# Three loads of v issued by ScalarE's queue instead of SyncE's, in a lightning-attention and MLP kernel

## Chip, cores and metric

The kernel runs on one core of one Trainium2 chip. The metric is the device time of one execution in microseconds (us); a number for a kernel is the median of its runs, in most cases four. A ratio is the mean time of one kernel's runs over the mean of the other's runs of the same rounds on the same chip, so it is not quite the ratio of the medians that are quoted; its 95% interval stands in brackets. The span in a profile is about 2 us shorter than the time of the same run. All times "at" a moment are us from the start of the span.

## The reference

A decayed linear attention over q, k and v of shape (4, 8, 768, 64), then an MLP with the tanh form of gelu over the 3072 x 512 result. Cut to what matters:

```python
# attention, in blocks of 64 rows, for each batch and head
intra = (qb @ kb.T) * Dmask                    # Dmask[i, j] = lam**(i-j) for i >= j
out   = intra @ vb + (qb * lam_pow) @ kv_state
kv_state = lam**64 * kv_state + (kb * rev_pow).T @ vb
...
x = out.transpose(0, 2, 1, 3).reshape(3072, 512)
# MLP
h = x @ w_in                                   # (512, 2048)
g = gelu_tanh(h)
return g @ w_out                               # (2048, 512), float32
```

## The kernel before

The attention is done in 24 steps; a step is 256 rows of four heads of one batch, and needs three loads (q, k, v) of 256 KB each, whose rows in memory are 512 bytes long. The weights are loaded in pieces whose rows are 2 KB long. SyncE issues nearly all of it, in this order: q, k, v of steps 0 to 3, w_in, w_out, q, k, v of steps 4 to 8. Only the small load of lam and v of step 0 go through ScalarE's queue.

```python
def load_step(s, names="qkv"):
    ...
        t = ld.tile([P, HH, 2, D], FP32, tag=nm + "32", name=f"{nm}32_{s}")
        rows = src[b, half * HH : (half + 1) * HH, sb * SB : (sb + 1) * SB, :]
        queue = nc.scalar if (nm, s) == ("v", 0) else nc.sync
        pin(queue.dma_start(out=t[:].rearrange("p h j d -> p h (j d)"),
                            in_=rows.rearrange("h (p j) d -> p h (j d)", j=2)))
...
def load_win(j, part=None):                    # part: half of the rows, for j = 0 and 1
    ...
    cs = slice(0, NC) if part is None else slice(2 * part, 2 * part + 2)
    pin(nc.sync.dma_start(out=t[:, cs, :], in_=src[:, cs, :]))
...
for s in range(4):
    load_step(s)
for j in range(4):
    for part in ((0, 1) if j < 2 else (None,)):
        load_win(j, part)
for j in (0, 2, 1, 3):
    load_wout(j)
for s in range(4, 9):
    load_step(s)
```

A step's inputs are then prepared: VectorE scales q (GpSimd does it in step 3), ScalarE casts k to 16 bits, GpSimd scales v into 16 bits. `stage_t` transposes q and k on TensorE and copies the result out of its banks; `scores`, `causal` and `products` follow. `idle(n)` issues n matmuls of no use, 0.22 us each at full clock, that keep TensorE busy. The front of the kernel, which is what the change touches:

```python
idle(4); prep(0); stage_t(0); idle(1)
square(5); square(6)
prep(1)
chunk_decay()
idle(2); R(0, None); stage_t(1); idle(5); U(0); prep(2)
scores(1); products(1, 0); causal(1); idle(1); stage_t(2); prep_qk(3)
...
idle(3); scores(2); products(2, None); update(2, 0); causal(2)
prep_v(3)                       # GpSimd: needs v of step 3
...
stage_t(3); products(None, 1); products(None, 2); ...
scores(3)
banks = products(3, None)       # TensorE: needs prep_v(3)
cast_win(0, 0, 256, 128, c01)   # VectorE: needs the first piece of w_in
...
queue_group(0)
fill(8)                         # TensorE: the first matmuls of the MLP
```

Each engine runs its instructions in this order. So the first MLP matmul can not start before `products(3, None)`.

## Time and profile before

| | before |
|---|---|
| median of runs | 204.0 us (203.85 to 204.35) |
| span of the profiled run | 202.2 us |
| TensorE busy | 194.2 us, 96% |
| first MLP matmul at | 16.82 us |
| second block of MLP matmuls at | 19.69 us |
| v of step 3 landed at | 13.76 us |
| cast of k of step 1 at | 7.57 us |

TensorE is nearly full from 17 us on, so the table follows the front only. The last two rows of TensorE to compare with later (the timeline of TensorE before; start, length, engine, line, operation, tiles, shapes, count, and in brackets the idle time before with what ended it):

```profile
16.82 2.36 PE L601 MATMUL Hps<-xT,w_in 128*128 128x256 f16 x20 [0.56 <-DVE w_in L108]
19.69 5.20 PE L601 MATMUL Hps<-xT,w_in 128*128 128x256 f16 x28
```

The first MLP matmul ended an idle time of 0.56 us, and what ended that was VectorE's cast of w_in.

### The profile page before, as it was taken

To read this page: it belongs to the slowest core of one execution; us is meant where nothing else is said; L and a number is where in the kernel's file an instruction comes from. 1 tells how busy PE (TensorE), PEld (TensorE's weight loads), DVE (VectorE), ACT (ScalarE), POOL (GpSimd) and SP (SyncE) were. 2 spreads that over 40 slices of the span, in tenths; PEclk is the share of its full clock that TensorE was granted. 3 is DMA by queue.
4 is the path that set the end of the run, shared out by engine and by line. 5 is a ranking of instruction groups with operands and counts; after the bars stand their busy time and mean duration, and the time that the engine had idled before them with its cause. 6 is when DMAs were issued, how large, how long until landed. Compare 5 with 4: busy or idle time off the path is not lost.

```text
span 202.2 us, 5666 instructions
## 1 busy us (share of the span) xinstructions
PE 194.2 (96%) x2348; PEld 130.1 (64%) x2348; DVE 145.7 (72%) x293; ACT 107.9 (53%) x205; POOL 66.3 (33%) x80
## 2 busy tenths in 40 slices
PE   6888999999999999999999999999999999999993
PEld 1456544456888888645688764589664688544882
DVE  5896623889999999967799749899566462334753
ACT  2475778375893473477642368614367424466210
POOL 6594123457458264162531609303302000000000
PEclk9999999999999999999999999999999999999999
DMA  5999999999999999999875999306510003300014
GB/s 170 291 327 387 387 387 378 286 291 320 334 239 216 272 233 235 210 277 200 205 182 127 243 285 218 45 0 138 132 51 3 0 0 107 104 0 0 3 45 163
DMA packets 64201, 37.85 MB, mean 187 GB/s; under 512 B 17584, under 2 KB 59568, under 8 KB 64176
## 3 DMA queue, kind: packets, MB, share of 16 engines
q1 hardware_dynamic: 63344, 36.97, 72.1%
q10 hardware_dynamic: 832, 0.52, 0.8%
q8 instruction: 18, 0.29, 0.6%
q14 instruction: 7, 0.06, 0.1%
HBM read 27.26 MB, written 6.29 MB: 166 GB/s over the span
## 4 chain that ended last, share of the span: by engine, by line
PE 81%; DVE 6%; SPq 4%; DMA 4%; ACT 2%; issue 2%; DVEq 0%
PE Hps L484 37%; PE MB L555 8%; PE MA L555 8%; PE MD L555 7%; SPq L70 4%; PE MC L555 4%; DMA wi<-in_moe_w_in_dram 4%; PE Hps L601 3%; PE O2ps L499 3%; PE S L295 3%; DVE w_sum L128 2%; PE OK L353 2%; PE OK L344 1%; PE Tps L266 1%; DVE gs L531 1%
## 5 line engine op out<-in xcount | busy, mean ns | idle before, releaser
L484 PE MATMUL Hps<-xT,w_in 128*128 128x512 f16 (+1 forms) x416 | 78.7, 346 | 0.0
L488 ACT ACTIVATE gT<-Hps 128x512 f16<-128x512 f32 x88 | 52.3, 597 | 29.1 <-PE Hps L484 28.3
L484 PEld LDWEIGHTS <-w_in 128*128 128x128 f16 x416 | 40.4, 98 | 33.7
L531 DVE TENSOR_TENSOR gs<-gT 128x1024 f16<-128x1024 f16 (+1 forms) x62 | 40.8, 712 | 18.3 <-ACT gT L488 18.3
L456 POOL TENSOR_TENSOR u<-t,lumask 128x256 f16<-128x256 f32 x40 | 29.4, 749 | 67.0 <-DVE t L449 49.6
L555 PEld LDWEIGHTS <-gs 128*128 128x128 f16 x400 | 39.0, 98 | 4.5
L305 DVE TENSOR_TENSOR PT<-S,mask 128x512 f16<-128x512 f32 x48 | 30.4, 682 | 9.5 <-PE S L295 9.5
L230 POOL TENSOR_TENSOR v<-v,dv 128x512 f16<-128x512 f32 x24 | 28.5, 1194 | 5.0 <-DMA v<-in_v_dram 4.5
L555 PE MATMUL MA<-w_sum,gT 128*128 128x256 f16 x160 | 19.5, 273 | 0.4 <-DVE o L587 0.3
L555 PE MATMUL MB<-w_out,gs 128*128 128x256 f16 x160 | 19.1, 273 | 0.0
L248 ACT ACTIVATE qk<-k 128x512 f16<-128x512 f32 x24 | 15.0, 625 | 7.6 <-DMA k<-in_k_dram 7.6
L562 ACT ACTIVATE m<-MB 128x512 f32<-128x512 f32 x10 | 6.0, 597 | 23.4 <-PE MB L555 23.4
L555 PE MATMUL MD<-w_sum,gs 128*128 128x256 f16 x152 | 18.4, 273 | 0.0
L555 PEld LDWEIGHTS <-gT 128*128 128x128 f16 x160 | 15.4, 98 | 3.5 <-ACT gT L488 0.5
L243 DVE TENSOR_TENSOR qk<-q,dq 128x512 f16<-128x512 f32 x23 | 17.6, 767 | 0.0
L430 ACT ACTIVATE xT<-OK 128x256 f16<-128x256 f32 x29 | 11.1, 453 | 8.2 <-PE OK L353 7.9
L499 PE MATMUL O2ps<-w_out,gT 128*128 128x512 f16 x64 | 14.6, 379 | 0.0
L566 DVE TENSOR_TENSOR o<-MA,m 128x512 f32<-128x512 f32 x10 | 6.9, 689 | 9.6 <-ACT m L562 9.6
L128 DVE TENSOR_TENSOR w_sum<-w_out 128x1024 f16<-128x1024 f16 x10 | 9.1, 947 | 6.3 <-POOL w_out L118 3.5
L430 ACT ACTIVATE xT<-O 128x256 f16<-128x256 f32 x18 | 6.4, 458 | 10.4 <-PE O L404 7.5
L295 PEld LDWEIGHTS <-qkT 64*64 64x64 f16 x384 | 6.0, 106 | 7.0 <-issue 3.2
L449 DVE SCALAR_TENSOR_TENSOR t<-t,lamu,OK 128x64 f32<-128x64 f32 x44 | 10.1, 273 | 0.5
(68 smaller groups left out, 168.8 us busy)
## 6 DMA issues: line engine op xcount, KB each, us to landing
q<-in_q_dram SPq DMA_DIRECT2D x24, 256.0 KB, 5.3
k<-in_k_dram SPq DMA_DIRECT2D x24, 256.0 KB, 5.2
v<-in_v_dram SPq DMA_DIRECT2D x23, 256.0 KB, 5.2
out_dram<-o SPq DMA_DIRECT2D x22, 256.0 KB, 4.5
wo<-in_moe_w_out_dram SPq DMA_DIRECT2D x4, 1024.0 KB, 9.6
wi<-in_moe_w_in_dram SPq DMA_DIRECT2D x4, 512.0 KB, 7.6
wi<-in_moe_w_in_dram SPq DMA_DIRECT2D x2, 1024.0 KB, 12.7
v<-in_v_dram ACTq DMA_DIRECT2D x1, 256.0 KB, 4.4
```

The source lines that it names most:

```text
L128: pin(eng.tensor_tensor(w_sum16[:, w_slot[m], 4 * j : 4 * j + 4, :], rows(f0, e0), rows(f1, e1), op))
L230: pin(nc.gpsimd.tensor_tensor(wide(tv[:]), ld32[s][2][:], decay(dv, s), ALU.mult))
L243: pin(q_eng.tensor_tensor(wide(tq), q32[:], decay(dq, s), ALU.mult))
L248: pin(nc.scalar.activation(out=wide(tk), in_=k32[:], func=AF.Copy))
L305: pin(nc.vector.tensor_tensor(t[:, hl].rearrange("p b c d -> p b (c d)"), Sps[:].rearrange("p b c d -> p b (c d)"), mask[:].unsqueeze(1).t ...
L430: pin(nc.scalar.activation(out=d, in_=o, func=AF.Copy))
L456: pin(nc.gpsimd.tensor_tensor(u[:], state[half][:].unsqueeze(2).to_broadcast([P, 2, 2, D]), lumask[:, 2 * half : 2 * half + 2, :].unsqueez ...
L484: pin(nc.tensor.matmul(by_block(Hps[:, i, :]), w_in16[:, c, f * P : (f + 1) * P], x(c), start=(c == 0), stop=(c == NC - 1)))
L488: pin(nc.scalar.activation(out=dst, in_=Hps[:], func=AF.Gelu_apprx_tanh))
L499: pin(nc.tensor.matmul(O2[tau][0][:], gT[:, f % HF, f // HF, tau * P : (tau + 1) * P], w_out16[:, f, :], start=(n == 0), stop=(n == NF - 1)))
L531: pin(nc.vector.tensor_tensor(gsum[m][:, i, :], block(T0, F0, i), block(T1, F1, i), op))
L555: pin(nc.tensor.matmul(dst, lhsT, rhs, start=(i == 0), stop=(i == HF - 1), skip_group_check=True))
```

## The change

The intent is to take issues off SyncE, so that w_in is asked for earlier, and to let v come through a second queue beside q and k. v of step 1 follows v of step 0 at the top. v of steps 2 and 3 are issued later, each behind a cast of k on ScalarE, and land in buffers of the output pool, which is unused then.

```diff
     ld32 = {}
+    v_ahead = {}
+
+    def load_tile(nm, s):
+        first = nm == "v" and s in (2, 3)
+        return (otp if first else ld).tile([P, HH, 2, D], FP32, tag="o32" if first else nm + "32",
+                                           name=f"{nm}32_{s}")
...
-            t = ld.tile([P, HH, 2, D], FP32, tag=nm + "32", name=f"{nm}32_{s}")
+            t = v_ahead.pop(s, None) if nm == "v" else None
+            if t is None:
+                t = load_tile(nm, s)
...
-            queue = nc.scalar if (nm, s) == ("v", 0) else nc.sync
+            queue = nc.scalar if nm == "v" and s < 4 else nc.sync
...
-    for s in range(4):
-        load_step(s)
+    load_step(0)
+    load_step(1)
+    for s in (2, 3):
+        load_step(s, "qk")
+        v_ahead[s] = load_tile("v", s)
...
     prep(0)
+    load_step(2, "v")
...
     prep(1)
+    load_step(3, "v")
```

## The prediction

> **What bounds the kernel now.** I read the page first. TensorE is busy 96% of the span, and its first four slices (5 us each) are the only ones clearly under nine tenths.
>
> ```profile
> span 202.2 us, 5666 instructions
> PE 194.2 (96%) x2348; PEld 130.1 (64%) x2348; DVE 145.7 (72%) x293; ACT 107.9 (53%) x205; POOL 66.3 (33%) x80
> PE   6888999999999999999999999999999999999993
> DMA  5999999999999999999875999306510003300014
> GB/s 170 291 327 387 387 387 378 286 291 320 334 239 216 272 233 235 210 277 200 205 182 127 243 285 218 45 0 138 132 51 3 0 0 107 104 0 0 3 45 163
> ```
>
> So after about 17 us the order of TensorE's own work sets the end, and what this change can move is the front: steps 0 to 3 of the attention, and the arrival of the first quarter of w_in. The DMA row says that the transfer engines are full from about 2.4 us on; the rate row says that loads of q, k and v run at about 290 GB/s and weights at about 387.
>
> Second, the chain that ended last, in order of time (start, length, what). It goes through SyncE's twelve issues, the load of w_in and its cast into the first matmul of the MLP.
>
> ```profile
> 8.46 0.83 SPq L70
> 9.33 7.12 DMA wi<-in_moe_w_in_dram
> 16.47 0.30 DVE w_in L108
> 16.82 2.36 PE Hps L601 x20
> ```
>
> It looks as if fewer issues ahead of 9.33 would bring w_in sooner. I do not believe that, for an issue of 0.83 us is about what 256 KB take at 290 GB/s (262144 / 290e3 = 0.90 us): SyncE waits there for room, not for its own work.
>
> Third, the timeline of ScalarE in the front (start, length, what, idle before).
>
> ```profile
> 1.82 1.28 ACT L184 ACT_TABLE_LOAD   x1 [1.82 <-issue]
> 5.12 0.63 ACT L248 ACTIVATE qk<-k 128x512 f16<-128x512 f32 x1 [1.81 <-DMA k<-in_k_dram]
> 7.57 0.63 ACT L248 ACTIVATE qk<-k 128x512 f16<-128x512 f32 x1 [1.81 <-DMA k<-in_k_dram]
> 8.69 1.02 ACT L273 ACTIVATE qkT<-Tps 128x1024 f16<-128x1024 f16 x1 [0.49 <-PE Tps L266]
> 10.26 0.63 ACT L248 ACTIVATE qk<-k 128x512 f16<-128x512 f32 x1 [0.55 <-DMA k<-in_k_dram]
> 12.99 0.63 ACT L248 ACTIVATE qk<-k 128x512 f16<-128x512 f32 x1 [0.78 <-DMA k<-in_k_dram]
> ```
>
> All four casts of k wait for their load: the front runs at the pace of arrivals. The waits by engine say the same of v: GpSimd waited 4.5 us for v in three waits, the longest 1.7 us, while ScalarE lost 7.6 us to k in six. In the timeline the front's last matmuls of TensorE end at about 16.3 us and the first MLP matmul starts at 16.82, after a cast that had waited for w_in until 16.45. The two paths therefore end within 0.5 us of each other. That is the most that an earlier w_in can give alone.
>
> **What the Trainium skill says.** "DMA: Bandwidth & Descriptors", section "Issuing engines are not separate DMA queues": DMAs from any engine run on the same 16 DMA engines and interleave, and a second issuer only saves sequencer time. Section "Queues, rings and completion order": each DMA engine takes the queues with work in turn, packet by packet. The trace agrees: from 3.5 to 4.5 us, when v of step 0 comes through ScalarE's queue (q10), the two queues moved 0.17 and 0.16 MB, an even share. It adds something: the sum was 324 GB/s then, against 288 from 5.5 to 6.5 us with one queue.
>
> ```profile
> DMA packets 645, 0.32 MB, mean 324 GB/s; under 512 B 13, under 2 KB 645, under 8 KB 645
> q1 hardware_dynamic: 341, 0.17, 56.1%
> q10 hardware_dynamic: 304, 0.16, 52.3%
> ```
>
> "Perfetto Trace Analysis", section "DMA Instruction — HWDGE (DVE, Sync)": the profiled time of an issue holds the wait for the descriptor generator's lock and the generation, not the movement. The trace has issues of 0.42 to 0.60 us on ScalarE at the start, and of 0.8 to 1.1 us on SyncE once it is full; what a ScalarE issue costs beside a full SyncE queue, no row of it shows.
>
> **The change part by part.** It removes no work. Three loads of 256 KB go from SyncE to ScalarE. Built, the changed kernel has the same order of instructions on TensorE, VectorE and GpSimd; SyncE has three fewer and ScalarE three more: v1 after v0, v2 after the cast of k0, v3 after the cast of k1. The eight completion semaphores are dealt round in order of issue, so that in the build the issue of v2 waits for the load of k1 to land, and that of v3 for q2. The cast of k1 stands behind the issue of v2.
>
> (a) Removed from SyncE: 0.51 + 0.83 + 0.83 = 2.2 us of issues ahead of w_in. Since the engines are full, nearly all of this is time spent waiting for room; I count none of it as gain.
>
> (b) Gained in bandwidth: three more loads shared with three of SyncE's, so six loads of 0.90 us each at some 10% more rate: about 0.5 us by the time that w_in has landed. Estimate: w_in at 15.7 to 16.2 instead of 16.45, or earlier still if it overtakes v3.
>
> (c) Lost for k1: before, k1 is fifth to arrive (landing at 7.55). Now v1 shares with q1 and k1, so k1 ends near the time when six loads (1.57 MB) have moved. Up to 3.5 us 0.30 MB have moved; then some 3.1 us at an estimated 335 GB/s while v0 and v1 share (1.05 MB), then 0.22 MB at 290 GB/s: 3.5 + 3.1 + 0.8 = 7.4, plus 0.7 from last packet to landing as k1 shows before: 8.1 us, 0.5 later.
>
> (d) Lost on ScalarE: behind that landing come the issue of v2 (0.45 if nothing is in its way) and only then the cast of k1; v3's issue (0.45) stands between that cast and the copy of step 1's transposed q and k. The cast ends near 9.2 instead of 8.2, the copy starts at 9.7 to 9.8 instead of 8.69: 1.0 to 1.1 us late.
>
> (e) Later arrivals: v2, issued at 8.1 and not at 5.6, lands at about 12.2 instead of 11.1 (1.9 us from issue to first packet as for v0, then 1.6 us at half rate, then 0.6). GpSimd does v2 (1.04 us) and then q3 (1.04), so the transposes of step 3 move from 13.43 to about 14.35. k2 and k3 come 0.3 to 0.7 earlier, which these delays hide.
>
> (f) Taken back: VectorE's masks of step 1 stood 0.6 us behind the scores before (10.82 against 10.2), so they slip by 0.5 only, and step 3's scores slip by about 0.6, from 15.7 to 16.3. TensorE's front then ends near 16.9, against w_in's cast near 16.6. First MLP matmul: 16.9 to 17.2, so 0.1 to 0.4 us later. After that TensorE has no idle time that would absorb it.
>
> Sum: 204.02 plus about 0.2: 204.2 us.
>
> **The rivals.** First, the generator is contended: SyncE is blocked on its full queue at 8 to 10 us, so the two ScalarE issues take 0.8 to 1.2 us each and not 0.45. For it: SyncE's own issues of that length. Against it: v0's issue of 0.42 beside SyncE's at the start, but then nothing was full. It adds 0.7 to 1.5 us to (d): 205 to 205.5. Second, the aim of the change comes true: v's bytes interleave without hurting k1, the shared rate is higher than I take it, and both the front and w_in are earlier. The gap of 0.5 us at 16.3 to 16.8 closes and perhaps 0.3 us more; the next bound is step 4's loads at 39 us (k4 lands about 38.8, its transposes start at 39.74). That makes 203.3 to 203.7. Third, it is all hidden and nothing moves: 204.0.
>
> **Range and chances.** The least that I see is 203.2, the most 205.5; first rival, second rival and the sum of my own steps get about a third each. Eight in ten: 203.2 to 205.2. A change of 2% would be 4.1 us, a quarter of the front; no path here gives that.
>
> **What would show it.** Right: k1's cast starts at 8.5 us or later; ScalarE's two late issues are seen at about 8.1 and 9.2; the rate between 5 and 7 us is above 310 GB/s; w_in's first cast is no longer preceded by a wait for its load; step 3's scores and the first MLP matmul start at 16.2 to 16.4 and 16.9 to 17.3; all of TensorE's later work keeps its length. Wrong: k1's cast at 7.6 us, or a first MLP matmul before 16.7; or a difference that arises after 20 us, where I expect a plain shift.

## More of the kernel before

On GpSimd, v of steps 2 and 3 had no wait at all in front of it (timeline of GpSimd before; no bracket means no idle time to speak of):

```profile
11.33 1.04 POOL L230 TENSOR_TENSOR v<-v,dv 128x512 f16<-128x512 f32 x1
14.48 1.04 POOL L230 TENSOR_TENSOR v<-v,dv 128x512 f16<-128x512 f32 x1
```

## The result, and the profile after

The changed kernel took 210.56 us at the median (209.95, 211.02, 211.27, 210.09) against 204.0: ratio 1.0324 [1.0294, 1.0354], slower by 3.2%. The prediction had said that no path gives a change of 2%, 4.1 us, and had put its most at 205.5 us. The page after:

```profile
span 207.8 us, 5665 instructions
...
PE   6895899999999999999999999999999999999993
...
DMA  6999789999999999959975999902720003200015
GB/s 173 292 348 374 237 280 320 353 273 285 338 323 224 188 264 246 253 137 220 253 155 157 230 221 212 202 0 34 176 101 5 0 0 104 96 5 0 3 35 167
```

The third slice (10.4 to 15.6 us) of the rate row rose from 327 to 348 GB/s while TensorE's fourth (15.6 to 20.8) fell from eight to five tenths: the transfers move more, and TensorE has less to do. Something moves early that is not yet needed. The timeline of TensorE names what it lacks:

```profile
18.05 0.32 PE L341 MATMUL OK<-v,qk 64*64 64x64 f16 x16 [1.39 <-POOL v L241]
...
21.94 0.32 PE L341 MATMUL OK<-v,qk 64*64 64x64 f16 x16 [0.67 <-POOL v L241]
22.19 2.66 PE L612 MATMUL Hps<-xT,w_in 128*128 128x256 f16 x20
...
25.37 4.99 PE L612 MATMUL Hps<-xT,w_in 128*128 128x256 f16 x27
```

The last product of step 3 waits for GpSimd's v, and the first MLP matmul, at 22.19 instead of 16.82 (+5.37), follows it without a wait. The second block is 5.68 later than before, the span 5.6 longer: all is lost before 26 us, and what follows is a shift. The timeline of GpSimd after shows what held v back:

```profile
16.96 1.04 POOL L241 TENSOR_TENSOR v<-v,dv 128x512 f16<-128x512 f32 x1 [4.09 <-DMA v<-in_v_dram]
...
20.85 1.04 POOL L241 TENSOR_TENSOR v<-v,dv 128x512 f16<-128x512 f32 x1 [0.71 <-DMA v<-in_v_dram]
```

It is the loads: v of step 2 landed at 16.87, v of step 3 at 20.78 (before: 13.76). Issued at 8.87 and 9.78, they took 8.0 and 11.0 us, where they had taken 5.5 and 5.3 before. ScalarE did its part close to the plan (its timeline after; ACTq is an issue of a DMA):

```profile
8.87 0.37 ACTq L78 DMA_DIRECT2D v<-in_v_dram  x1
9.29 0.63 ACT L259 ACTIVATE qk<-k 128x512 f16<-128x512 f32 x1 [3.25 <-DMA k<-in_k_dram]
9.78 0.38 ACTq L78 DMA_DIRECT2D v<-in_v_dram  x1
10.62 1.02 ACT L284 ACTIVATE qkT<-Tps 128x1024 f16<-128x1024 f16 x1 [0.70 <-PE Tps L277]
```

What v met on the way is in the DMA view of 13 to 18 us, after (queue, packets, MB, share of the 16 engines; q1 is SyncE's queue, which then carries w_in, q10 ScalarE's, which carries v):

```profile
DMA packets 1462, 1.80 MB, mean 360 GB/s; under 512 B 54, under 2 KB 769, under 8 KB 1461
...
q1 hardware_dynamic: 727, 1.42, 79.6%
q10 hardware_dynamic: 734, 0.37, 26.9%
```

The two queues moved nearly the same number of packets, 727 and 734. But a packet of w_in is a row of 2 KB (1.42 MB / 727 = 1950 bytes) and one of v a row of 512 bytes (0.37 MB / 734 = 504). So v got 0.37 of 1.79 MB, one fifth of the rate: 0.37 MB in 5 us is 74 GB/s, and 512 KB at 74 GB/s take 7 us. Before, v of step 3 stood in SyncE's queue ahead of w_in and had the whole rate.

One caution for reading this trace: TensorE's front ran at half speed until 14.48 us, where the trace first records a full clock (before: at 4.83). The granted clock that the windows of the profile give reads 1.00 for the stretch ahead of that record too, but the durations tell it. Five filling matmuls, the first line before and the second after (timelines of TensorE):

```profile
8.49 1.24 PE L155 MATMUL idle<-ones 128*128 128x512 f16 x5
10.37 2.34 PE L166 MATMUL idle<-ones 128*128 128x512 f16 x5
```

A second profile of the changed kernel (l_after_again below) had full speed from 4.55 us on and lost as much, so this is not the cause of the loss.

w_in profited: its first piece landed at 13.8 instead of 16.45. That was of no use, for its cast stood behind the delayed front and did not wait for the load (timeline of VectorE after; no bracket):

```profile
21.06 1.60 DVE L116 CAST w_in<-wi 128x256 f16<-128x256 f32 x2
```

### The profile page after: what moved, and what is told of

It is laid out like the page before. It is cut to its first block, busy times and chain, and to the rows that moved or that the text cites. A ratio compares the mean times of both kernels' runs of the same rounds, so it can differ in the third digit from the quotient of the medians. Undisturbed runs are those within 1.5% of the kernel's fastest.

```text
span 207.8 us, 5665 instructions
## 1 busy us (share of the span) xinstructions
PE 197.8 (95%) x2348; PEld 132.0 (64%) x2348; DVE 147.3 (71%) x293; ACT 108.0 (52%) x205; POOL 67.1 (32%) x80
## 4 chain that ended last, share of the span: by engine, by line
PE 80%; DVE 8%; issue 4%; DMA 3%; POOL 2%; ACT 1%; SPq 0%; POOLq 0%; DVEq 0%
PE Hps L495 36%; PE MB L566 8%; PE MA L566 7%; PE MD L566 7%; PE O2ps L510 5%; PE MC L566 4%; PE Hps L612 3%; DMA q<-in_q_dram 3%; PE S L306 2%; DVE PT L316 2%; PE OK L364 2%; PE OK L355 1%; POOL u L467 1%; PE Tps L277 1%; DVE gs L542 1%
## 5 line engine op out<-in xcount | busy, mean ns | idle before, releaser
L467 POOL TENSOR_TENSOR u<-t,lumask 128x256 f16<-128x256 f32 x40 | 30.1, 764 | 69.1 <-DVE t L460 49.8
L316 DVE TENSOR_TENSOR PT<-S,mask 128x512 f16<-128x512 f32 x48 | 30.4, 682 | 10.4 <-PE S L306 10.4
L566 PE MATMUL MD<-w_sum,gs 128*128 128x256 f16 x152 | 18.4, 273 | 0.0
L441 ACT ACTIVATE xT<-O 128x256 f16<-128x256 f32 x18 | 6.4, 459 | 10.4 <-PE O L415 7.5
```

The lines of the kernel that those rows point to most:

```text
L316: pin(nc.vector.tensor_tensor(t[:, hl].rearrange("p b c d -> p b (c d)"), Sps[:].rearrange("p b c d -> p b (c d)"), mask[:].unsqueeze(1).t ...
L441: pin(nc.scalar.activation(out=d, in_=o, func=AF.Copy))
L467: pin(nc.gpsimd.tensor_tensor(u[:], state[half][:].unsqueeze(2).to_broadcast([P, 2, 2, D]), lumask[:, 2 * half : 2 * half + 2, :].unsqueez ...
L566: pin(nc.tensor.matmul(dst, lhsT, rhs, start=(i == 0), stop=(i == HF - 1), skip_group_check=True))
```

## The experiments

The theory after reading the traces: v of step 3 crosses with w_in in the second queue, and its share by turns of packets costs some 4 to 5 us. Rivals: the order of ScalarE's issues and casts delays k and with it everything; the sharing of v of step 1 costs it; or part of the loss is TensorE's clock, which the trace sometimes shows at half after a long wait. Fourteen runs, in four groups, each group on one chip beside the kernel before (203.8 to 204.4 us there):

| label | what | median us | ratio to before | first MLP matmul at |
|---|---|---|---|---|
| a_only_v1 | before, v1 on ScalarE | 205.29 | 1.0081 [1.0044, 1.0119] | 18.13 |
| b_only_v23 | changed, v1 back on SyncE | 209.96 | 1.0302 [1.0280, 1.0324] | 20.71 |
| c_v_at_top | before, v0 to v3 on ScalarE, all at the top | 206.22 | 1.0133 [1.0088, 1.0178] | 18.13 |
| e_sync_behind_k | v2, v3 on SyncE, behind k3, ahead of w_in | 205.65 | 1.0087 [1.0063, 1.0111] | 18.85 |
| f_only_v2 | v2 alone behind the cast of k0 | 205.97 | 1.0087 [1.0045, 1.0130] | 18.25 |
| g_wi_1KB | changed, w_in in rows of 1 KB at first | 208.86 | 1.0223 [1.0168, 1.0278] | 22.24 |
| h_b_warm | b, TensorE kept busy in its wait | 208.10 | 1.0177 [1.0138, 1.0216] | 20.66 |
| i_k01_scalar | before, k0 and k1 on ScalarE, all v on SyncE | 205.49 | 1.0065 [1.0019, 1.0112] | 18.13 |
| l_after_again | changed, again | 211.44 | 1.0374 [1.0318, 1.0429] | 22.51 |
| j_after_warm | changed, 8 filling matmuls | 211.78 | 1.0361 [1.0315, 1.0406] | 24.13 |
| k_b_1KB | b, w_in in rows of 1 KB at first | 208.80 | 1.0234 [1.0201, 1.0268] | 19.99 |
| m_before_1KB | before, w_in in rows of 1 KB at first | 207.21 | 1.0133 [1.0078, 1.0188] | 17.36 |
| n_after_warm10 | changed, 12 filling matmuls | 210.23 | 1.0326 [1.0251, 1.0400] | 21.92 |
| o_hold_wi | changed, w_in held until v3 has landed | 208.17 | 1.0176 [1.0130, 1.0221] | 20.81 |

v0 to v3 stand for v of steps 0 to 3, and k and q likewise. The last column is from the one profiled run of each; it need not follow the median where the clock differs from run to run. By the rule of this study, which calls a difference clear from 2% on, a, c, e, f, i and m are the same as before, g, h and o are unclear, and the rest are slower; the intervals of all of them lie above 1, so the smaller losses are read from those.

### a_only_v1: the first part of the change alone

```diff
-queue = nc.scalar if (nm, s) == ("v", 0) else nc.sync      # before
+queue = nc.scalar if nm == "v" and s < 2 else nc.sync
```

> Only v1 moves to ScalarE's queue; v2 and v3 stay on SyncE ahead of w_in. Theory S (the small packets of v2 and v3 starve beside the large ones of w_in): no v load is left beside w_in, so nearly all of the loss is gone: 203.5 to 205.0 us, v2 and v3 landing at 11 to 14 us. Theory K (v1 takes half of the rate from q1 and k1, k1 is late and TensorE's clock stays low): the loss stays, 207 us or more, with the cast of k1 at 8.8 us or later.

Measured: 205.29 us, 1.0081. k1 landed at 9.04 instead of 7.55 and was cast at 9.06 instead of 7.57; the first MLP matmul was at 18.13, 1.3 later. So v1 in the second queue costs 1.3 to 1.7 us, a little more than theory S had allowed (205.0 at most), by making k1 late; it is not the 6.5 us.

### b_only_v23: the other two parts alone

```diff
-queue = nc.scalar if nm == "v" and s < 4 else nc.sync      # changed
+queue = nc.scalar if nm == "v" and s in (0, 2, 3) else nc.sync
```

> v1 goes back to SyncE; v2 and v3 come through ScalarE's queue behind the casts of k. Theory S: at least 4 of the 6.5 us stay (208 to 211 us), v2 lands at 15 us or later and v3 at 18 or later, with about as many packets on ScalarE's queue as on SyncE's while both are at work. Theory K: k1 is back at 7.6 us and the loss shrinks to 1.5 us or less (205.5 or less).

Measured: 209.96 us, 1.0302, nearly the whole loss, although k1 was cast at 7.88, as early as before within 0.3 us. v2, issued at 7.45, landed at 12.75 (15 or later had been expected), for it was nearly ahead of w_in: q10 moved 460 packets from 11 to 12 us, q1 only 98. v3, issued at 9.23, landed at 19.33, 10.1 us later. That tells v3 apart from v2 and from k (timeline of GpSimd):

```profile
19.37 1.04 POOL L241 TENSOR_TENSOR v<-v,dv 128x512 f16<-128x512 f32 x1 [3.32 <-DMA v<-in_v_dram]
```

In this run TensorE's wait was unbroken, and something else came to light: the first block of MLP matmuls, 2.36 us long before, took 3.86 (timeline of TensorE, then its stretch from 21 to 25 us with the columns length, busy time of PE, PEld, DVE, ACT and POOL with counts, granted clock, DMA share, GB/s):

```profile
20.46 0.32 PE L341 MATMUL OK<-v,qk 64*64 64x64 f16 x16 [3.29 <-POOL v L241]
20.71 3.86 PE L612 MATMUL Hps<-xT,w_in 128*128 128x256 f16 x20
```

```profile
21.00:25.00 4.00, 4.00 (x36) 2.72 (x35) 1.84 (x5) 0.00 (x0) 1.18 (x2) 0.57 0.96 301
```

The granted clock was half from 21.37 to 24.78 us, which is 3.41 us.

### c_v_at_top: ScalarE's queue, but all issues at the top

```diff
-queue = nc.scalar if (nm, s) == ("v", 0) else nc.sync      # before
+queue = nc.scalar if nm == "v" and s < 4 else nc.sync
```

> All three v loads on ScalarE's queue, but issued at the top, before the table load, in the buffers of before. Theory S: ScalarE's queue holds its small packets beside SyncE's small packets of q and k, the shares are even, v3 lands by 13 us and before w_in: 203.5 to 205.5 us. Theory A (issues on ScalarE block its casts): its first four issues hold ScalarE until about 5 us, the cast of k0 starts late, loss of 1 to 2 us. Theory K: 207 us or more, as k1 is later still than in the change.

Measured: 206.22 us, 1.0133, above the 205.5 of theory S. The same four loads through the same queue, and most of the loss is gone: they ran beside q and k of 512-byte rows and were done before w_in. ScalarE's issues ended at 3.5 us and the cast of k0 was on time (5.04). k1 and k2 came late (cast at 8.97 and 12.23), and a loss of 1.3% stays, which is not clearly more than a's. So the bulk is not the queue itself but what the queue meets, and that depends on the time of issue.

### e_sync_behind_k: late in the order, but on SyncE and ahead of w_in

```diff
-queue = nc.scalar if nm == "v" and s < 4 else nc.sync      # changed
+queue = nc.scalar if nm == "v" and s < 2 else nc.sync
...
     v_ahead[s] = load_tile("v", s)
+for s in (2, 3):
+    load_step(s, "v")
...
-load_step(2, "v")      # behind prep(0)
-load_step(3, "v")      # behind prep(1)
```

> v1 on ScalarE as in the change; v2 and v3 as late in the order as there, behind k3, but on SyncE ahead of w_in. Theory S: v2 lands at about 12.5 and v3 at about 13.7 us, the loss is 0.5 to 2 us (204.5 to 206). If instead the order alone (v behind k) were the cause, it stays at 209 us or more.

Measured: 205.65 us, 1.0087, the same as a within the intervals. v2 landed at 13.46 and v3 at about 14.4 (before: 11.1 and 13.76), both later, and this cost nothing that shows beside a. The two still landed in the buffers of the output pool, so these are not the cause either. What matters for v is to be ahead of w_in.

### f_only_v2: the second part alone, v3 ahead of w_in

```diff
-queue = nc.scalar if nm == "v" and s < 4 else nc.sync      # changed
+queue = nc.scalar if nm == "v" and s in (0, 2) else nc.sync
...
-load_step(3, "v")      # behind prep(1); instead load_step(3) at the top
```

> As b_only_v23, but v3 goes on SyncE behind k3 and ahead of w_in; only v2 comes through ScalarE's queue behind the cast of k0. Theory S puts the loss on v3, the one load that still ran beside w_in in that run (v2 had landed at 12.8 us, before w_in's packets): v3 lands near 13.8 us, 204.0 to 205.3 us. If the late issue itself (the waits on ScalarE, the cast of k1 behind the issue) were the cause, 206 or more.

Measured: 205.97 us, 1.0087, outside the 204.0 to 205.3 of theory S and just short of the 206 that the rival had been given. So the late issue has a cost of its own, some 2 us, but v2 on ScalarE is cheap as long as v3 stays on SyncE: between b and f only v3 moves, and 4 us go with it. The part that v2 costs comes in a way that the diff does not show (timeline of ScalarE):

```profile
8.33 0.45 ACTq L78 DMA_DIRECT2D v<-in_v_dram  x1
8.83 0.63 ACT L259 ACTIVATE qk<-k 128x512 f16<-128x512 f32 x1 [3.17 <-DMA v<-in_v_dram]
```

The eight completion semaphores are dealt in order of issue, and here v2's issue got that of v1: it waited until v1 had landed (8.29), and the cast of k1 stood behind it. An issue put between two pieces of ScalarE's work can inherit a wait for somebody else's load, as here.

### g_wi_1KB, k_b_1KB and m_before_1KB: the size of w_in's rows

If turns go by packet, w_in in rows of half the length must leave v a larger share. The first four of w_in's loads, 512 KB each, were cut by columns instead of by rows, so that their rows are 1 KB:

```diff
-pin(nc.sync.dma_start(out=t[:, cs, :], in_=src[:, cs, :]))
+fs = slice(0, 512)
+if part is not None:
+    cs, fs = slice(0, NC), slice(256 * part, 256 * part + 256)
+pin(nc.sync.dma_start(out=t[:, cs, fs], in_=src[:, cs, fs]))
```

> The changed kernel with one thing different: the first four loads of w_in are cut by columns, so that a contiguous piece is 1 KB and not 2 KB (same bytes, same number of loads, same order). Theory S (the two queues take turns by packet, so the share of bytes follows the packet sizes): v's share of the bytes rises from about 0.20 to about 0.33, v2 lands at about 15.2 us instead of 16.9 and v3 at about 18 instead of 20.8, and the kernel is faster than the changed one by 1.5 to 3 us (207.5 to 209) although w_in itself loads no faster. If v2 and v3 are late for another reason (late issue, order), nothing moves by more than 0.5 us.

> b_only_v23 with the first four w_in loads cut into pieces of 1 KB. There q1, k1 and v1 are on time, so that v3 alone is beside w_in. Theory S: v3 takes about 8 us from issue to landing instead of 10.1, lands at about 17.3 us instead of 19.3, and the time falls by 1.5 to 3 us from 210.0. If the packet size doesn't matter, v3 lands at 19.3 again and the time stays at 210.

> Control: the kernel before with the same cut of w_in. No v load runs beside w_in there, so smaller pieces can't help: 203.8 to 205.5 us, rather slower, since the first matmul now needs both column halves.

Measured, the share: in k_b_1KB from 14 to 16 us (DMA view),

```profile
q1 hardware_dynamic: 434, 0.43, 69.5%
q10 hardware_dynamic: 430, 0.22, 41.8%
```

again as many packets from each queue, and now v has one third of the bytes; in b from 14 to 17 us it was 0.22 of 1.07 MB with 436 and 439 packets. The cause of the share beside w_in is shown by that: the packets stay equal, and the bytes follow the row. In g it is less even, 352 to 455 packets and 0.17 to 0.45 MB from 14 to 16 us.

Measured, the time: v3 took 9.0 us in k (10.1 in b) and landed at 18.4 instead of 19.33; 17.3 had been expected. In g it took 9.4 (11.0 in the changed kernel), but k1 was late in that run (cast at 10.95), v2 was issued at 10.53 only, and v3 landed at 20.8 as in the changed kernel, not at 18; the profile of g shows no gain at the first MLP matmul. g came to 208.86 and k to 208.80 us, 1.7 and 1.2 us less than the medians of the kernels they are made from; k's fall is short of the 1.5 to 3 us expected. The control m missed its range: the cut alone costs the kernel before 1.3%, 207.21 us. The pieces then arrive in an order that its casts wait for (an idle time of 1.00 us within the first MLP matmuls), and half clock from 19.29 to 22.70 us followed. Against that control, g is slower by 1.7 us and k by 1.6 where their uncut forms are slower by 6 to 6.5 (medians, from different chips; the kernel before lay within 0.5 us between these). This is less clean than the packet counts, since m's loss by late w_in need not add to a loss by late v.

### h_b_warm: what of b is the clock

```diff
 scores(3)
+idle(12)
```

added to b, so that the wait for v3 is filled with matmuls of no use.

> b_only_v23 with twelve matmuls of no use on TensorE behind step 3's scores, where it waits for v3 from 17.2 to 20.5 us. If the 3.4 us at half clock that followed this wait (21.4 to 24.8 us) are a cost of their own, they go and the time falls by 1.2 to 1.7 us (208.3 to 208.9). If they cost nothing, it stays at 210.0.

Measured: 208.10 us, 1.0177, against b's 209.96 (1.0302). v3 was as late as in b (landed at 19.28), and the first MLP matmul stood at the same place, but it then ran at full clock:

```profile
17.05 2.76 PE L166 MATMUL idle<-ones 128*128 128x512 f16 x12
...
20.66 2.36 PE L612 MATMUL Hps<-xT,w_in 128*128 128x256 f16 x20
```

```profile
21.00:25.00 4.00, 3.90 (x50) 3.05 (x48) 3.06 (x10) 0.80 (x2) 1.58 (x3) 1.00 0.84 299
```

Here 50 matmuls fit into the 4 us where b had 36, and the next MLP block was at 23.53 instead of 25.20. So 1.9 us of b's loss are the clock (by the medians, from different chips; the intervals of b and h do not meet), and the rest, 1.8%, is the wait itself: 20.66 against 16.82 is 3.84 us, and the ratio gives 3.6.

### i_k01_scalar: the second queue for k instead of v

```diff
-queue = nc.scalar if (nm, s) == ("v", 0) else nc.sync      # before
+queue = nc.scalar if nm == "k" and s < 2 else nc.sync
```

> Not the change: k0 and k1 instead of v0 come through ScalarE's queue, all v on SyncE. If a second queue helps whichever load the front waits for next, k1 lands at 6.3 to 7.0 us instead of 7.5 and the time falls by 0.1 to 0.5 us (203.3 to 203.9). If the second queue is harmful as such, 204.5 or more.

Measured: 205.49 us, 1.0065: a miss, on the side of the other expectation (204.5 or more). k1 landed at about 8.2, not at 6.3 to 7.0. An attempt to turn the second queue to use for what the front waits for did not beat the kernel before.

### l_after_again, j_after_warm and n_after_warm10: the clock in the changed kernel

The changed kernel's first profile had no drop of the clock once it was full, at 14.48 us, but the other three of its four runs had a mean granted clock of 0.982 to 0.984. It was therefore profiled again, and run with filling matmuls.

```diff
 scores(2)
+idle(5)       # j_after_warm;  n_after_warm10: idle(10)
 ...
 scores(3)
+idle(3)       # j_after_warm;  n_after_warm10: idle(2)
```

> The changed kernel once more, on the same chip as the three runs beside it, so that they can be compared with it directly: 210 to 211.3 us.

> The changed kernel with five matmuls of no use behind step 2's scores and three behind step 3's, in the two gaps in which TensorE waits for v2 and v3. If part of the loss is TensorE's clock, which drops after such gaps (h_b_warm: 1.9 us), the time falls by 0.7 to 1.5 us against the changed kernel of the same rounds (209.0 to 209.9). If it is the wait for v alone, it stays within 0.4 us of it.

> As j_after_warm, with ten matmuls of no use behind step 2's scores and two behind step 3's. The five of j filled 1.1 of a gap of 3.4 us and the clock dropped all the same. If the dropped clock (18.2 to 25.0 us in the profile of l_after_again) is a cost of its own in the changed kernel, the time now falls to 208.8 to 210.2 us and the profile shows full clock from 15 us on; if not, 210.5 or more.

Measured: l had half clock from 18.2 to 25.03 us, 6.83 us long, after TensorE had waited 3.42 us for v2 (its stretch of 18 to 25 us, columns as above, clock 0.51):

```profile
18.00:25.00 7.00, 6.32 (x98) 4.58 (x91) 5.75 (x14) 3.11 (x7) 4.67 (x7) 0.51 0.89 323
```

Its next MLP block was at 26.59 against 25.37 in the first profile, 1.2 us later. In the first profile TensorE had reached the wait for v2 late, being slow until 14.48 us, had waited 1.39 us and not 3.42, and no drop followed. j's filling was too short: the clock still dropped at 18.37, the last three filling matmuls then took 1.46 us at half clock in the way of step 3's last product, and j gained nothing (211.78). n's profile had the full clock from 5.09 on and that block at 24.80, but its four runs (209.26 to 212.37) lie around the changed kernel's, ratio 1.0326 [1.0251, 1.0400]. So in the changed kernel the cost of the clock is seen in traces, 1.2 us between two profiles, and is not shown by an intervention; in b it is.

### o_hold_wi: v as in the change, w_in held back

The last test takes away what v2 and v3 meet, and leaves them where the change has put them. All loads of weights and of steps 4 to 8 are moved behind a small copy out of v3's buffer on SyncE's queue, so that none is issued before v3 has landed:

```diff
 load_step(3, "v")      # behind prep(1), as changed
+hold = const.tile([P, 2 * D], FP32)
+pin(nc.sync.dma_start(out=hold[:], in_=ld32[3][2][:, 0].rearrange("p j d -> p (j d)")))
+...                    # here load_win, load_wout, load_step(4..8), taken from the top
```

> The changed kernel, with all w_in, w_out and later loads on SyncE held until v3 has landed (by a small copy out of v3 ahead of them). v2 and v3 are still issued by ScalarE, v3 still behind the cast of k1 (v2 may go a little earlier, as the semaphores fall otherwise). Theory S: without w_in beside it v3 lands at 13.5 to 14.5 us instead of 20.8, and although w_in starts some 6 us later than in the changed kernel, the time falls to 205 to 207.5 us. If the late issue or ScalarE's queue as such were the cause, v3 is late again, w_in later still, and the time is over 211.

Measured: 208.17 us, 1.0176, faster than the changed kernel but not the 205 to 207.5 expected. v3, issued at 9.91, had landed by 15.09, in at most 5.2 us and not 11.0 (timeline of SyncE):

```profile
15.09 0.55 SPq L698 DMA_DIRECT2D hold<-v  x1
15.68 3.46 SPq L100 DMA_DIRECT2D wi<-in_moe_w_in_dram  x6
```

w_in was issued at 15.68 instead of 7.82, and its first piece landed at 20.38. The first MLP matmul was at 20.81, right behind the last product of step 3 (20.51 and 0.29 us long), and its cast of w_in had waited 0.17 us: now both paths ended together. Neither waited for v3, which GpSimd took up at 18.99. The front itself was late, with k1 cast at 9.90 and TensorE at half speed until 15.98 us in this profile. Asking for the weights 8 us later made the changed kernel faster by 1.5% (1.0324 to 1.0176), and gave v3 its old time. One thing differs besides: the semaphores fell otherwise, so that v2 was issued at 4.98 already. v2 took 8.0 us here too, with no w_in about, behind v1 and beside the q and k of SyncE; so the eight microseconds of v2 in the changed kernel are not put down to w_in alone. For v3, the pair stands.

No version beat the kernel before.

## Why the prediction was wrong, point by point

**What bounds the kernel: right in kind, short in reach.** TensorE's order after 17 us set the end, and the change acted through the front; the loss was a plain shift from 26 us on. The front was taken as the two paths that ended within 0.5 us of each other. The path through v of step 3 had slack: it landed at 13.76 and GpSimd took it up at 14.48, so 0.7 us there. It was never asked what would happen to that load.

**(a) right.** Fewer issues on SyncE gained nothing: w_in was issued 1.5 us earlier and no step of the chain moved forward by it.

**(b) wrong, and read upside down.** The shared rate was 286 GB/s from 5.5 to 6.5 us (DMA view after), not above 310:

```profile
DMA packets 576, 0.29 MB, mean 286 GB/s; under 512 B 17, under 2 KB 576, under 8 KB 576
```

The 324 GB/s that the prediction took from 3.5 to 4.5 us before did not carry over. Nor was the share in that window even, as the prediction read it: v0 comes in only midway. From 4 to 5 us, before, with 512-byte rows in both queues, the second queue moved nearly twice the packets of the first:

```profile
q10 hardware_dynamic: 439, 0.22, 75.9%
q1 hardware_dynamic: 235, 0.11, 40.8%
```

The view of 5.5 to 6.5 us after has 348 against 228. Equal turns are what the traces show beside w_in, from 13 us on, and not everywhere; why is open. Worse, w_in overtaking v3 was counted as a gain, and it was the mechanism of the loss.

**(c) right in direction, too small.** k1's load reached its end at 8.84, 1.3 later, where 0.5 was expected. The missing rate of (b) explains most of that: 1.05 MB at 286 and not 335 GB/s take 0.5 us more. (By 3.5 us the trace before has moved 0.36 MB, not the 0.30 of the prediction's sum; that alone would bring k1 forward by 0.2.) Run a shows what it costs when it is not hidden: 0.8%, as against "about 0.2 us" for the whole change. In the changed kernel it is mostly hidden behind v3: b without it lost nearly as much.

**(d) right in its durations.** The issues took 0.37 and 0.38 us, the cast of k1 started at 9.29, and the copy of the transposed q and k at 10.62 instead of 9.7 to 9.8, after the later landing of k1. The first rival, issues of 0.8 to 1.2 us by a contended generator, is refuted by the two durations.

**(e) is the step that failed.** It says that v2 has "1.9 us from issue to first packet as for v0, then 1.6 us at half rate, then 0.6", and lands at about 12.2. It landed at 16.87: issued at 8.87, it had its first row at 12.17, after 3.3 us and not 1.9, its rows took until about 16.3, so 4.1 us and not 1.6, and the landing 0.5 (the trace's packet records). And v3, issued 0.9 us after v2 into the same queue, with w_in filling the other, got no number at all. The prediction had quoted that turns go by packet, and had the sizes of the rows at hand: 512 bytes and 2 KB. That gives one fifth, not one half, for as long as w_in runs, and w_in's 4 MB outlast v by far. Worked with it: the rate of some 360 GB/s leaves v 72, and the 512 KB of v2 and v3 need 7 us, from about 12 us on; that is an estimate of 19, where the trace has 20.78. The runs that show it: b, with v3 at 10.1 us from issue to landing and 1.0302; f, where v3 alone is put back ahead of w_in, 1.0087; k, where shorter rows change the share of bytes and not of packets; o, where v3 without w_in takes at most 5.2 us.

**(f) fell with it.** The front's last product ended at 22.26 instead of 16.26, 6.0 us later and not 0.6, and the first MLP matmul came 5.4 us later and not 0.1 to 0.4; w_in's cast waited for none of its loads, as the prediction had expected, but for the reason that everything else was late. "No path here gives that", of 2%, was wrong, because the list of rivals held none in which a moved load loses its place, and none in which TensorE's clock drops.

**The second cost, missed as well.** A wait of 3.3 us in front of TensorE was followed by half clock for 3.41 us. In b this is 1.9 us of the 6.2. "TensorE: Matmul & The Clock Gate" of the Trainium skill, section "What's actually happening", has the idle window of about 3.4 us after which the clock is halved. The traces agree in that length, with stretches of half clock of 3.41 us in b and 6.83 us, twice as much, in l, but not in how idle TensorE must be: the wait in b was 3.29 us, and shorter ones were followed by half clock too (see the list at the end). The kernel's `idle` calls keep TensorE busy in the waits of the kernel before; they do not cover these longer ones.

**Open.** The share is not all of v3's 11.0 us. A load's end is marked in the packet records by sixteen packets of 4 bytes, and the load landed about 0.5 us after the last of them. For v3 in the changed kernel thirteen came between 17.82 and 18.40 us, near the estimate above, and the last three at 19.42, 19.83 and 20.29. In b fifteen came by 17.19 and the last at 18.82, in k by 16.43 and at 17.94; in o, without w_in, fourteen came by 13.05 and the last at 14.55. So 1.5 to 1.9 us of v3's time are a few late parts, with w_in or without; why they lag is not known. Nor is it known why v2 in the changed kernel waited 3.3 us and v3 in b 4.3 us from issue to first row, when their queue was empty. How much of v2's 8.0 us is due to w_in is open too (see o). What the clock costs in the changed kernel is bracketed by traces alone.

## What to carry to other kernels

A load's place in a full queue can be worth more than its time of issue: moved to a second queue, it no longer stands ahead of what comes after it in the first, and shares with that by turns. Work out the share in bytes from the rows of both sides before moving it, and ask for each moved load how much slack its first use has. And when TensorE's front becomes late by as much as here (waits of 3.3 and 3.4 us in b and l), add the clock's share: the work after the wait ran at half speed for 3.4 to 6.8 us, so the wait was paid more than once.

## What the Trainium skill lacked or had wrong

- "DMA: Bandwidth & Descriptors", section "Queues, rings and completion order", has the turns by packet but not what follows for two queues with rows of different length. The runs show that, beside w_in, the packets are equal or nearly so and the bytes follow the row: 727 to 734 packets with 1.42 to 0.37 MB (rows of 2 KB and 512 bytes), 434 to 430 packets with 0.43 to 0.22 MB (rows of 1 KB and 512 bytes). With 512-byte rows in both queues the turns were not even: 235 to 439 packets from 4 to 5 us before. The packets of the trace hold one row each; several descriptors to a packet, as the section has it, can not be seen in it.
- The same page, section "Issuing engines are not separate DMA queues", says that several issuers only save time on the sequencer. The runs show that a second issuer can also cost: 3.2% for the whole change and 4 us between b and f, by the place that the load gives up.
- No page says what rate two busy queues reach with loads like these: 324 GB/s at 3.5 to 4.5 us before, but 286 at 5.5 to 6.5 after, no more than one queue alone (288).
- "Perfetto Trace Analysis", section "DMA Instruction — HWDGE (DVE, Sync)", speaks of a wait for the generator's lock within the issue. Beside a full SyncE queue, ScalarE's late issues took 0.37 to 0.38 us (0.45 in f): no such wait showed.
- "TensorE: Matmul & The Clock Gate", section "What's actually happening", puts half clock after at least one idle window of about 3.4 us. The length fits (3.41 us of half clock in b), but the runs show the drop after less idleness: in m half clock (19.29 to 22.70 us) followed 3.41 us in which TensorE was busy for 1.97, with 1.00 us as the longest gap. The section does not say how little work counts as idle.
